# The channel layer of a three-stage kernel by seven block products instead of eight, with the weights' sums on GpSimd and a new order of the program

## Chip, cores and metric

One core of a Trainium2 chip. The metric is the device time of one execution in microseconds (us). The kernel before takes 362.83 us (median of three runs, 362.69 to 362.89).

## The reference

Three stages follow each other on a batch of 2 sequences of 768 tokens with 512 features (8 heads of 64).

```python
# stage 1: retention, by head
state = gamma * state + k_t v_t^T ;  y_t = scale * q_t state
# stage 2: mixing of tokens, then the channel layer
theta = x @ w_theta
y = w_tok_r @ (x * cos(theta)) + w_tok_i @ (x * sin(theta))
u = x + y
x = u + maximum(u @ w_ch, 0)
# stage 3: gated block
h = gelu(x @ w_in) ;  u, v = halves of h
v_n = (v - mean) / sqrt(var + 1e-6) * g_ln
gated = u * (w_sg @ v_n + b_sg)
out = x + gated @ w_out
```

The line that the change works on is `u @ w_ch`.

## The kernel before

**Numbers.** Every operand of a large product is split into two parts of type fp32r, a high half (ScalarE copies the tile, `split_hi`, L339) and a low half (VectorE subtracts the high half from the tile, `split_lo`, L345). `terms3` (which calls `mm`, L319) makes one product of three matmuls: high by high, low by high, high by low.

**Tiling.** Tokens stand in the columns. Group 0 is the first 512 tokens of batch 0, group 1 the first 512 of batch 1, group 2 the last 256 of both. The features are four tiles of 128 rows, so x (`xa` for groups 0 and 1, `xb` for group 2) has tiles (g, d) of 128 x 512. A call of `layer` makes one output tile of 128 x 512 from four input tiles: 4 x 3 = 12 matmuls of 512 columns into one of 8 PSUM banks.

**Stages in the code.** `retention` works through 12 chunks of 128 tokens (scores, mask, outer product, state, attend), `theta` makes the angle and z = x cos, x sin of a chunk, `mix_main` and `mix_rest` mix the tokens (`mix_main` the first 512 columns, in four banks, with matmuls of 512 columns; `mix_rest` the last 256, with matmuls of 256 columns). The last chunk's `mix_main` is followed by `add` (L830), which makes u, and by the halves of u (`split_x` into `uhl`). `channels` is the channel layer, one call of `layer` for each group and feature tile, then `relu` (L908) and the halves of the result (`x2hl`). `up_four`, `up_u` and `up_v` are the first layer of stage 3, `gate_tile` the mixing with w_sg, `finish_four` and `finish` the last layer.

**Seven products.** `up_four` and `finish_four` make the tiles of groups 0 and 1 of their layers by `seven`: the weights (two blocks of input features by two of output features) and the tokens (two blocks of input features by groups 0 and 1) form a 2 x 2 block product. `sum_weights` forms four sums of weight blocks (VectorE, L1138), `sum_tokens` four differences of token tiles for each of two tile numbers (VectorE, L1158), each with its two halves. `seven` makes seven products of 6 matmuls each in four banks, `both` (ScalarE L1202, VectorE L1207) adds two of them into a buffer, and three more adds give the other results.

**Order of the work.** Every step is recorded as an operation of an engine with what it reads and writes. The list `ORDER` gives the sequence, `Plan.schedule` assigns the buffers in that sequence and the instructions are issued in it, each engine in its own order. SP issues all loads and stores but one (`load_half` L465, `weight` L400, the decays are issued by ScalarE). `weight` loads 1 MB of a weight pair and prepares it: L411 on ScalarE, L421 and L431 on VectorE, then the two halves. Before `WARM` a few small matmuls on the identity keep PE busy in its planned gaps (`keep_warm`).

Of the kernel before, what the change touches and what calls it, by code (L numbers as in the profile page):

```python
# [14 lines left out]
ALU = mybir.AluOpType  # L15
# [50 lines left out]
class Plan:  # L66
# [105 lines left out]


ORDER = [
# [52 lines left out]
]  # L227


# [1 line left out]
def retention_spectral_gmlp(  # L231
# [579 lines left out]
    def mix_main(b, s, prio):  # L811
# [14 lines left out]
        if s == NCH - 1:  # L826
            for d in range(NP):

                def add(d=d):
                    V.tensor_tensor(  # L830
                        out=x_tile(b, d), in0=ap(y[b, d]), in1=x_tile(b, d), op=ALU.add
                    )

                t = prio + 1 + d * 0.1
                dve(512, add, ps=True, r=[y[b, d]], w=x_keys(b, d), prio=t)
                split_x(uhl, b, d, t + 1 + LATE * (1 - b))

    def mix_rest(b, s, prio):
        i = b * NCH + s
# [59 lines left out]

    x2hl = {}  # L900

    def channels(g, e, prio):

        t = layer(W_CH, uhl, g, e, prio)

        def relu():
            u = x_tile(g, e)
            V.scalar_tensor_tensor(  # L908
                out=u, in0=ap(t), scalar=0.0, in1=u, op0=ALU.max, op1=ALU.add
            )  # L910

        dve(512, relu, ps=True, r=[t], w=x_keys(g, e), prio=prio)
        split_x(x2hl, g, e, prio)

    def gelu(t, o, prio, ps=True):

# [198 lines left out]
    def sum_weights(base, prio):  # L1115
# [17 lines left out]
            (lambda: block(0, 1), lambda: s3(1), ALU.subtract, [1]),  # L1133
        ]
        for i, (x, y, op, of) in enumerate(pairs):
            dve(
                512,
                lambda i=i, x=x, y=y, op=op: V.tensor_tensor(out=s3(i), in0=x(), in1=y(), op=op),  # L1138
                r=[plain[base][1], plain[base + 1][1], *(sums[n] for n in of)],
                w=[sums[i]],  # L1140
                prio=prio,
            )
            res.append(pair())
            split(res[i], lambda i=i: ap(sums[i]), 512, prio, [sums[i]])
# [90 lines left out]
        dma(256, put, r=[o], prio=prio)  # L1235

    def up_four(j, ws, ts, prio):
        z, x, y, u, v = seven(W_INU, x2hl, ws, ts, j, prio)
        for g, f, part in ((0, j, z), (1, j, x), (0, 2 + j, y), (1, 2 + j, v)):
            if f % 2 == 0:  # L1240
                gu[g, f], gu[g, f + 1] = halves()
            t = part
            if part is not z:
                t = v if part is v else Buf()
                dve(
                    512,
                    lambda t=t, part=part: V.tensor_tensor(
                        out=ap(t), in0=ap(part), in1=ap(u), op=ALU.add
                    ),
                    ps=part is not v, r=[part, u], w=[t], prio=prio,  # L1250
                )
            gelu(t, gu[g, f], prio, ps=part is z)

    def finish_four(j, ws, ts, prio):
        z, x, y, u, v = seven(W_OUT, ghl, ws, ts, j, prio)
# [94 lines left out]
    for k in range(2):  # L1350
        weight(W_INU + k, t - 10 + 5 * k)
        weight(W_INV + k, t + 30 + 5 * k)
    for g in range(3):
        for e in range(NP):
            channels(g, e, t)
            t += 2.7
    ws = sum_weights(W_INU, t - 8)
    ts = sum_tokens(lambda g, d: (lambda: x_tile(g, d), x_keys(g, d)), t - 4)
    for f in range(NP):
# [144 lines left out]
```

## Time and profile before

| | |
|---|---|
| median of the runs | 362.83 us |
| the profiled execution's own time | 362.86 us |
| its span (first to last instruction) | 361.1 us |
| PE (matmul) busy | 356.1 us, 99%, 2308 instructions |
| VectorE (DVE) busy | 295.5 us, 82%, 476 |
| ScalarE (ACT) busy | 187.0 us, 52%, 314 |
| GpSimd (POOL) busy | 9.0 us, 3%, 18 |
| moved by DMA | 44.33 MB |
| granted TensorE clock | 1.00 throughout |

Busy times are unions of the instructions' times on one engine. Matmuls overlap each other, and their ends are modelled, so PE's busy share says that PE always has something under way and not at which pace; the pace is read from the starts. A row of a group names the code line, the engine, the operation, what it writes and reads, the count, the busy time and the mean time of one in ns, and the idle time before it with what ended it.

### The profile page before, as it was taken

What the parts mean: (1) busy time and instruction counts of PE and PEld (TensorE: products, weight loads), DVE (VectorE), ACT (ScalarE), POOL (GpSimd) and SP (SyncE); (2) the same over time, 40 slices, a digit from 0 to 9 for tenths busy, and PEclk for the clock granted to TensorE, in tenths of its full rate; (3) what the DMA queues carried; (4) which work ended last, traced back from release to release, by engine and by line L of the source; (5) the groups of instructions that cost most, each with busy time, mean ns of one, the idle gap of its engine ahead of it and who ended that gap; (6) DMA issues with size and microseconds to landing.
All of it is one profiled execution on the core that took longest, in us unless ns stands there. A gap on an engine that the chain in (4) does not pass through costs nothing.

```text
span 361.1 us, 5762 instructions
## 1 busy us (share of the span) xinstructions
PE 356.1 (99%) x2308; PEld 305.0 (84%) x2308; DVE 295.5 (82%) x476; ACT 187.0 (52%) x314; POOL 9.0 (3%) x18
## 2 busy tenths in 40 slices
PE   8999999999999999999999999999999999999996
PEld 8878888888999888889988888888888889988885
DVE  2799989899478798952788788799899979989984
ACT  1689895545255458524532365465588651342310
POOL 1110000010001000002000000000000000000000
DMA  7999675435773155056023000011000000000224
GB/s 297 416 408 414 259 238 214 182 116 175 239 269 141 54 193 159 0 218 235 0 118 116 0 2 0 0 30 60 0 0 3 0 1 2 2 0 0 72 104 174
DMA packets 13946, 44.33 MB, mean 123 GB/s; under 512 B 1760, under 2 KB 5344, under 8 KB 11488
## 3 DMA queue, kind: packets, MB, share of 16 engines
q1 hardware_dynamic: 13776, 43.92, 33.2%
q8 instruction: 18, 0.29, 0.3%
q14 instruction: 8, 0.07, 0.1%
q10 hardware_dynamic: 144, 0.05, 0.1%
HBM read 38.19 MB, written 5.77 MB: 122 GB/s over the span
## 4 chain that ended last, share of the span: by engine, by line
PE 93%; DMA 4%; DVE 1%; ACT 1%; issue 0%
PE banks L319 93%; DMA xb<-wts 3%; DMA dec<-decays 1%; DVE xb L431 0%; DVE b L345 0%; ACT xb L411 0%; ACT b L339 0%; PE banks L760 0%; DVE b L1311 0%
## 5 line engine op out<-in xcount | busy, mean ns | idle before, releaser
L319 PE MATMUL banks<-b,b 128*128 128x512 f32 (+2 forms) x1764 | 323.0, 350 | 0.5 <-DVE b L345 0.5
L319 PEld LDWEIGHTS banks<-b,b 128*128 128x128 f32 (+1 forms) x1764 | 274.2, 183 | 47.3 <-issue 1.9
L339 ACT ACTIVATE b<-b 128x512 fp32r<-128x512 f32 (+1 forms) x83 | 63.4, 788 | 72.0 <-PE banks L319 26.4
L345 DVE TENSOR_TENSOR b<-b,b 128x512 fp32r<-128x512 f32 (+1 forms) x83 | 70.8, 873 | 14.4 <-ACT b L339 8.9
L345 DVE TENSOR_TENSOR b<-xa,b 128x512 fp32r<-128x512 f32 (+1 forms) x26 | 18.5, 726 | 10.2 <-ACT b L339 10.2
L339 ACT ACTIVATE b<-xa 128x512 fp32r<-128x512 f32 (+1 forms) x26 | 16.9, 663 | 14.0 <-DVE xa L908 5.6
L511 DVE TENSOR_TENSOR b<-banks,causal 128x512 f32<-128x512 f32 x24 | 16.2, 684 | 7.1 <-PE banks L319 7.1
L411 ACT ACTIVATE b<-b 128x1024 f32<-128x1024 f32 x16 | 18.2, 1149 | 5.0 <-DMA b<-wts 4.9
L431 DVE SCALAR_TENSOR_TENSOR b<-b 128x1024 int32<-128x1024 int32 x16 | 19.7, 1228 | 1.2 <-ACT b L411 0.9
L319 PE MATMUL banks<-b 64*128 64x128 f32 (+1 forms) x352 | 19.4, 256 | 0.2
L319 PEld LDWEIGHTS banks<-b 64*128 64x128 f32 (+1 forms) x352 | 17.3, 165 | 2.2 <-DMA b<-qkv 0.8
L938 ACT ACTIVATE b<-b 128x512 f32<-128x512 f32 x24 | 14.6, 627 | 6.7 <-DVE b L928 6.7
L534 ACT ACTIVATE b<-b,dec 128x64 f32<-128x64 f32 x56 | 14.1, 335 | 6.4 <-DMA b<-qkv 6.4
L920 ACT ACTIVATE b<-banks 128x512 f32<-128x512 f32 x18 | 10.2, 589 | 9.3 <-PE banks L319 9.1
L928 DVE SCALAR_TENSOR_TENSOR b<-b,banks 128x512 f32<-128x512 f32 x18 | 12.1, 678 | 2.1 <-ACT b L920 1.9
L421 DVE TENSOR_SCALAR b<-b 128x1024 int32<-128x1024 int32 x16 | 11.0, 686 | 3.2 <-DMA b<-wts 3.2
L339 ACT ACTIVATE b<-xb 128x512 fp32r<-128x512 f32 (+1 forms) x13 | 8.4, 665 | 9.5 <-DVE xb L866 7.8
L782 DVE TENSOR_TENSOR b<-b,b 128x512 f32<-128x512 f32 x20 | 13.2, 680 | 0.1
L716 ACT ACTIVATE b<-banks 128x512 int32<-128x512 f32 x12 | 7.1, 589 | 11.8 <-PE banks L319 11.8
L1029 ACT ACTIVATE b<-b,rstd 128x512 f32<-128x512 f32 x12 | 9.6, 806 | 5.7 <-DVE rstd L1018 5.7
L944 DVE SCALAR_TENSOR_TENSOR b<-b,banks 128x512 f32<-128x512 f32 x18 | 11.9, 679 | 0.6 <-ACT b L938 0.4
L1202 ACT ACTIVATE b<-banks 128x512 f32<-128x512 f32 x8 | 4.7, 593 | 14.2 <-PE banks L319 13.0
(75 smaller groups left out, 217.6 us busy)
## 6 DMA issues: line engine op xcount, KB each, us to landing
b<-wts SPq DMA_DIRECT2D x16, 1024.0 KB, 5.1
b<-qkv SPq DMA_DIRECT2D x24, 512.0 KB, 9.7
out<-b SPq DMA_DIRECT2D x11, 256.0 KB, 2.1
scr<-b SPq DMA_DIRECT2D x5, 512.0 KB, 4.6
b<-scr SPq DMA_DIRECT2D x20, 128.0 KB, 3.1
b<-wsg SPq DMA_DIRECT2D x9, 256.0 KB, 7.4
xa<-wts SPq DMA_DIRECT2D x2, 1024.0 KB, 11.9
xb<-wts SPq DMA_DIRECT2D x1, 1024.0 KB, 10.6
```

What stands on the lines that cost most here:

```text
L319: nc.tensor.matmul(out=o, lhsT=l, rhs=r, start=start, stop=stop, skip_group_check=more)
L339: act(words, lambda: A.activation(out=hi(), in_=src(), func=AF.Copy), prio=prio, r=r, **k)
L345: lambda: E.tensor_tensor(out=lo(), in0=src(), in1=hi().bitcast(F32), op=ALU.subtract),
L411: lambda: A.activation(out=words(1).bitcast(F32), in_=words(1).bitcast(F32), func=AF.Prelu, scale=REBIAS, alpha=SIGN_UP,),
L421: lambda: V.tensor_scalar(out=words(0), in0=words(0), scalar1=29, scalar2=None, op0=ALU.logical_shift_right),
L431: lambda: V.scalar_tensor_tensor(out=words(0), in0=words(1), scalar=3, in1=words(0), op0=ALU.logical_shift_left, op1=ALU.bitwise_or,),
L511: V.tensor_tensor(out=ap(at[i])[:, h * 512 + lo : h * 512 + hi].rearrange("p (n t) -> p n t", n=n), in0=ap(sc[h])[:, lo:hi].rearrange("p ( ...
L534: A.activation(out=v, in_=v, func=AF.Copy, scale=dk[:, h : h + 1])
L782: V.tensor_tensor(out=v, in0=x, in1=v, op=ALU.mult)
L928: lambda: V.scalar_tensor_tensor(out=ap(s), in0=ap(s), scalar=1.0 / GA, in1=ap(t), op0=ALU.add, op1=ALU.mult),
L938: lambda: A.activation(out=ap(s), in_=ap(s), func=AF.Tanh, scale=GA * GC),
L944: lambda: V.scalar_tensor_tensor(out=ap(o), in0=ap(s), scalar=1.0, in1=ap(t), op0=ALU.add, op1=ALU.mult),
```

## The change

1. The channel layer of groups 0 and 1 is made by `seven` too, as `channels_four`; group 2 stays with `channels`. The adds after `seven` move to a helper `sums_of` that `up_four` uses as well. `relu` becomes a function of its own.
2. The halves of u of batch 1 are made only for the feature tiles 2 and 3 (`seven` doesn't use the other two).
3. The four sums in `sum_weights`, now called for three layers, are formed by GpSimd (`pool`, G.tensor_tensor) instead of VectorE.
4. `ORDER` is another list (1059 operations instead of 1007).

```diff
@@ ORDER
-    48, 50, 62, 49, 63, 105, 51, 106, 0, 52, 168, 118, 64, 53, 119, 55, 54, 56, 6, 67, 58, 57, 66,
...
+    48, 49, 50, 55, 52, 56, 118, 63, 62, 105, 106, 119, 51, 0, 120, 53, 54, 168, 58, 64, 181, 67,
...
@@ mix_main
-                split_x(uhl, b, d, t + 1 + LATE * (1 - b))
+                if b == 0 or d >= 2:
+                    split_x(uhl, b, d, t + 1 + LATE * (1 - b))
@@ channels
+    def relu(g, e, t, ps, prio):
+        u = x_tile(g, e)
+        dve(
+            512,
+            lambda: V.scalar_tensor_tensor(
+                out=u, in0=ap(t), scalar=0.0, in1=u, op0=ALU.max, op1=ALU.add
+            ),
+            ps=ps, r=[t], w=x_keys(g, e), prio=prio,
+        )
+        split_x(x2hl, g, e, prio)
+
     def channels(g, e, prio):
...
+        relu(g, e, layer(W_CH, uhl, g, e, prio), True, prio)
+
+    def channels_four(j, ws, ts, prio):
+        for g, e, t, ps in sums_of(seven(W_CH, uhl, ws, ts, j, prio), j, prio):
+            relu(g, e, t, ps, prio)
+
+    def sums_of(parts, j, prio):
+
+        z, x, y, u, v = parts
+        yield 0, j, z, True
+        for g, e, part in ((1, j, x), (0, 2 + j, y), (1, 2 + j, v)):
+            t = v if part is v else Buf()
+            dve(
+                512,
+                lambda t=t, part=part: V.tensor_tensor(
+                    out=ap(t), in0=ap(part), in1=ap(u), op=ALU.add
+                ),
+                ps=part is not v, r=[part, u], w=[t], prio=prio,
+            )
+            yield g, e, t, False
@@ sum_weights
-            dve(
+            pool(
                 512,
-                lambda i=i, x=x, y=y, op=op: V.tensor_tensor(out=s3(i), in0=x(), in1=y(), op=op),
+                lambda i=i, x=x, y=y, op=op: G.tensor_tensor(out=s3(i), in0=x(), in1=y(), op=op),
@@ the main program
-    for g in range(3):
-        for e in range(NP):
-            channels(g, e, t)
-            t += 2.7
+    ws = sum_weights(W_CH, t - 30)
+    ts = sum_tokens(lambda g, d: (lambda: x_tile(g, d), x_keys(g, d)), t)
+    for j in range(2):
+        channels_four(j, ws, ts, t)
+        t += 9.5
+    for e in range(NP):
+        channels(B, e, t)
+        t += 2.7
```

What the new list does to the order shows at three places. Line numbers of the changed kernel are 4 to 25 higher there.

**SP, the first loads.** `b<-qkv` are the halves of retention chunks, `xb<-wts` is the first pair of theta weights (it lands in the space of xb), `dq` the query decays. Before:

```order
L465 DMA b_102<-qkv 128x1024
L465 DMA b_105<-qkv 128x1024
L465 DMA b_107<-qkv 128x1024
L465 DMA b_109<-qkv 128x1024
L465 DMA b_111<-qkv 128x1024
L490 DMA dq<-qdecays 128x512
L465 DMA b_114<-qkv 128x1024
L400 DMA xb<-wts 128x2048
```

Now:

```order
L469 DMA b_102<-qkv 128x1024
L469 DMA b_105<-qkv 128x1024
L469 DMA b_107<-qkv 128x1024
L469 DMA b_109<-qkv 128x1024
L469 DMA b_111<-qkv 128x1024
L469 DMA b_113<-qkv 128x1024
L469 DMA b_115<-qkv 128x1024
L469 DMA b_117<-qkv 128x1024
L494 DMA dq<-qdecays 128x512
L404 DMA xb<-wts 128x2048
```

Eight loads of chunks stand ahead of the theta weights where six stood, and the query decays come after all eight.

**PE, the last work ahead of the first theta product.** Rows `banks<-b` of 128x128 are scores, of 64x64 outer products, rows with 64x128 are attends, `banks<-ident,xa` is a transpose, 128x512 is theta. Before:

```order
L319 MATMUL banks<-b_114 64x64 x8
L760 MATMUL banks<-ident,xa_88 128x128 x4
L319 MATMUL banks<-b_111,state_66 64x128 x8
L319 MATMUL banks<-b_200,b_114 64x128 x8
L319 MATMUL banks<-b_128 128x128 x8
L319 MATMUL banks<-b_130 128x128 x8
L319 MATMUL banks<-b_273,b_202 128x512 x2
```

Now:

```order
L323 MATMUL banks<-b_117 64x64 x8
L323 MATMUL banks<-b_107,state_67 64x128 x8
L323 MATMUL banks<-b_176,b_117 64x128 x8
L323 MATMUL banks<-b_146 128x128 x8
L323 MATMUL banks<-b_165 128x128 x8
L323 MATMUL banks<-b_179 128x128 x8
L764 MATMUL banks<-ident,xa_88 128x128 x4
L323 MATMUL banks<-b_327,b_280 128x512 x2
```

Two more scores, one more outer product and one more attend have come ahead of the first theta product.

**DVE, after the last products of main mixing.** L830 (now L834) are the adds that make u, L345 (now L349) low halves, L1183 the new token differences. Before:

```order
L830 TENSOR_TENSOR xa_89<-banks,xa_89 128x512 x2
L345 TENSOR_TENSOR b_1691<-xa_89,b_1691 128x512
L345 TENSOR_TENSOR b_1689<-b_1590,b_1689 128x512
L345 TENSOR_TENSOR b_1705<-b_1541,b_1705 128x512
L830 TENSOR_TENSOR xa_89<-banks,xa_89 128x512
```

Now:

```order
L834 TENSOR_TENSOR xa_89<-banks,xa_89 128x512
L1183 TENSOR_TENSOR b_1666<-xa_89 128x512
L349 TENSOR_TENSOR b_1625<-b_1615,b_1625 128x512
L1183 TENSOR_TENSOR b_1671<-xa_89 128x512
L349 TENSOR_TENSOR b_1669<-b_1666,b_1669 128x512
L349 TENSOR_TENSOR b_1688<-b_1671,b_1688 128x512
L349 TENSOR_TENSOR b_1582<-xa_88,b_1582 128x512
L1183 TENSOR_TENSOR b_1704<-xa_88,b_1623 128x512
```

Where halves of u followed the adds, differences and their halves now stand; the first product on a difference reads `b_1688`.

## Rows read from the trace of the kernel before

**Rows 1.** The page's first part: busy us (share) x instructions of each engine.

```profile
PE 356.1 (99%) x2308; PEld 305.0 (84%) x2308; DVE 295.5 (82%) x476; ACT 187.0 (52%) x314; POOL 9.0 (3%) x18
```

**Rows 2.** The chain that ended last: start us, us, what.

```profile
4.77 10.56 DMA xb<-wts
...
15.36 1.22 ACT xb L411
...
16.60 1.24 DVE xb L431
...
17.86 1.18 ACT b L339
...
19.06 1.24 DVE b L345
...
20.34 18.55 PE banks L319 x226
38.89 0.59 PE banks L760 x4
39.48 318.51 PE banks L319 x1840
357.99 0.02 issue
358.01 0.42 DVE b L1311
```

**Rows 3.** PE's timeline (start us, us), then groups by form (busy us, mean ns).

```profile
199.83 15.35 PE L319 MATMUL banks<-b,b 128*128 128x512 f32 x67
...
L319 PE MATMUL banks<-b,b 128*128 128x512 f32 x1116 | 256.7, 390 | 0.5 <-DVE b L345 0.5
```

**Rows 4.** Groups by form on DVE and ACT, then a pair in DVE's timeline.

```profile
L345 DVE TENSOR_TENSOR b<-b,b 128x512 fp32r<-128x512 f32 x55 | 36.2, 685 | 2.8 <-ACT b L339 2.8
L339 ACT ACTIVATE b<-b 128x512 fp32r<-128x512 f32 x55 | 33.2, 627 | 51.5 <-PE banks L319 16.8 <-DVE b L1106 15.4 <-DVE b L1158 9.2
...
192.77 1.28 DVE L345 TENSOR_TENSOR b<-b,b 128x512 fp32r<-128x512 f32 x2
```

**Rows 5.** Stretches: us, busy us (x) PE, PEld, DVE, ACT, POOL; clock, DMA, GB/s.

```profile
10.00:40.00 30.00, 29.39 (x383) 24.57 (x382) 27.33 (x41) 25.19 (x68) 2.82 (x4) 1.00 1.02 412
...
160.00:260.00 100.00, 100.00 (x510) 85.71 (x509) 78.30 (x134) 48.04 (x80) 2.32 (x2) 1.00 0.17 61
```

**Rows 6.** Timeline, POOL beside DVE, at 48.9 and at 74.2 us.

```profile
48.90 0.61 POOL L578 TENSOR_TENSOR state<-grown,dec 128x256 f32<-128x256 f32 x1 [20.04 <-PE banks L319]
...
74.23 0.68 DVE L345 TENSOR_TENSOR b<-xa,b 128x512 fp32r<-128x512 f32 x1
74.46 0.93 POOL L578 TENSOR_TENSOR state<-grown,dec 128x256 f32<-128x256 f32 x1 [24.95 <-DVE grown L575]
74.83 1.64 DVE L345 TENSOR_TENSOR b<-b,b 128x1024 fp32r<-128x1024 f32 x1
...
77.00 1.21 DVE L345 TENSOR_TENSOR b<-b,b 128x1024 fp32r<-128x1024 f32 x1
```

**Rows 7.** Timeline of the tail, PE's last matmuls of 256 columns.

```profile
355.77 2.20 PE L319 MATMUL banks<-b,b 128*128 128x256 f32 x17
```

**Rows 8.** Timeline of PE in the head (x8 in the order is x16 here).

```profile
5.15 2.06 PE L319 MATMUL banks<-b 64*128 64x128 f32 x32
...
7.16 0.94 PE L319 MATMUL banks<-ident 128*128 128x128 f32 x6
...
8.54 1.14 PE L319 MATMUL banks<-b,b 128*64 128x128 f32 x16
...
20.34 2.56 PE L319 MATMUL banks<-b,b 128*128 128x512 f32 x10 [0.53 <-DVE b L345]
...
28.14 1.09 PE L319 MATMUL banks<-b,state 64*64 64x128 f32 x16
29.16 1.09 PE L319 MATMUL banks<-b,b 128*64 128x128 f32 x16
30.09 0.64 PE L319 MATMUL banks<-b 128*64 128x64 f32 x16
30.65 5.73 PE L319 MATMUL banks<-b,b 128*128 128x512 f32 x24
```

More of the change, by code (lines that the diff above doesn't have):

```diff
@@ L900, in retention_spectral_gmlp @@
     x2hl = {}
-    def channels(g, e, prio):
[L904 to L909, printed above, removed]
-            )
-        dve(512, relu, ps=True, r=[t], w=x_keys(g, e), prio=prio)
-        split_x(x2hl, g, e, prio)
+    def relu(g, e, t, ps, prio):
[8 more added lines that the diff above has]
+        split_x(x2hl, g, e, prio)
+    def channels(g, e, prio):
+        relu(g, e, layer(W_CH, uhl, g, e, prio), True, prio)
[13 more added lines that the diff above has]
+                ps=part is not v, r=[part, u], w=[t], prio=prio,
+            )
+            yield g, e, t, False
     def gelu(t, o, prio, ps=True):
@@ L1237, in up_four @@
     def up_four(j, ws, ts, prio):
-        z, x, y, u, v = seven(W_INU, x2hl, ws, ts, j, prio)
-        for g, f, part in ((0, j, z), (1, j, x), (0, 2 + j, y), (1, 2 + j, v)):
+        for g, f, t, ps in sums_of(seven(W_INU, x2hl, ws, ts, j, prio), j, prio):
             if f % 2 == 0:
                 gu[g, f], gu[g, f + 1] = halves()
[L1242 to L1252, printed above, removed]
+            gelu(t, gu[g, f], prio, ps=ps)
     def finish_four(j, ws, ts, prio):
```

106 rows, old and new, of the table ORDER are left out of this document.

## Prediction, made before the changed kernel was run

> **What bounds the kernel now.** The page's first part comes first: TensorE (PE) is busy for 99% of the span, VectorE (DVE) for 82%, ScalarE for 52%, GpSimd for 3% [rows 1]. The chain that ended last says the same in order of time: from 20.34 us to 357.99 us there is nothing but PE in it, before that the load and the preparation of the first theta weights, after it one DVE add and the store [rows 2]. A busy PE need not be a full PE, so I looked at its pace: 67 matmuls of 512 columns took 15.35 us [rows 3], and with the last one's shown 0.39 us taken off, the 66 steps are 0.227 us each. All 1116 such matmuls at that pace are 253 us [rows 3], and after 20.34 us the trace knows no wait of PE but the 0.53 us that end there [rows 8]. So the reader should see a kernel whose time is (moment at which PE becomes gapless) + (PE's remaining work) + (tail of 361.1 - 357.99 = 3.1 us). The change can gain only by taking away PE work or by making PE gapless earlier, and it can lose by any new wait of PE.
>
> **Fewer products.** The channel layer for groups 0 and 1 was 2 x 4 calls of `layer`, 12 matmuls each, 96 in all. Now it is 2 x 7 products of 6 matmuls, 84. Twelve matmuls of 512 columns go: 12 x 0.227 = **2.72 us** [rows 3]. Group 2 keeps its four `layer` calls, the other layers keep theirs. This is on the path, since PE is.
>
> **What the other engines get for it.** DVE gets 8 token sums and their 8 low halves, loses 2 low halves of u (batch 1, tiles 0 and 1), gets 4 low halves of the weight sums, 4 adds in `both`, 6 in `sums_of`, and loses the 8 weight sums of the two later layers: net 20 instructions of 512 columns. One alone shows 0.68 us, two in a row 1.28 us, so one more costs 0.60 us [rows 4]: 20 x 0.60 = 12.0 us. ScalarE gets 14 copies (8 - 2 + 4 high halves, 4 in `both`) at about 0.63 us [rows 4], 8.8 us, where 48% of PE's section is used [rows 5]; I count nothing for it, and if that cover were gone the chains of `split` would be 0.6 us later each. GpSimd gets 12 sums. Its row has 256 columns, 0.61 us undisturbed [rows 6], so 512 columns are 1.22 us by twice that, and 0.61 us if it were all fixed cost; I take 1.22, 14.7 us in all. Nothing waits for a weight sum at short notice: the order puts each behind its weights and many DVE instructions ahead of its product. SP issues the same number of transfers.
>
> **Is DVE still ahead of PE?** In the stretch from the end of mixing to the first layer's activations (160 to 260 us) PE is busy 100.0 us and DVE 78.3 us [rows 5]. Of the instructions above 24 net fall here (the 4 sums of the output weights that leave DVE lie later): 78.3 + 24 x 0.60 = 92.7 us against a PE stretch of 100 - 2.7 = 97.3 us. That is tight but under. I walked the new order at the places where PE first needs DVE. Take t = 0 at the end of the last product of main mixing. PE then has four groups of 12 matmuls of 256 columns, 12 x 0.12 us each by the tail's row (17 take 2.20 us, the last one's overlap included, [rows 7]), so the first product on a token difference is due at 5.8 us. DVE has the last mixing add, two differences and three low halves up to the one needed, six instructions of 0.60 us, and with ScalarE's copy between they are done at about 4 us. It is 1.8 us early. The second product is due at 10.0 us, its low half stands seven instructions further, at 8.1 us. The channel results of group 2 and the next layer's differences I walked the same way: the margins are 1 to 3 us, the smallest 0.6 us near the end, where the last tile of the gate passes through DVE. The thing that hides the 12 us is thus DVE's idle time; once it is gone, each DVE instruction costs its 0.60 us.
>
> **GpSimd against DVE.** Where a GpSimd product overlapped DVE instructions with two SBUF inputs, both lost time: GpSimd took 0.93 us instead of 0.61, and the DVE instruction behind it 1.64 us instead of 1.21 [rows 6]. So 0.2 to 0.4 us of DVE were lost per GpSimd instruction of 0.61 us, when DVE was two-input work at that moment, and nothing when it read PSUM. For 12 sums of twice the length that is 0 to 12 x 0.8 = 9.6 us of DVE time; I take the middle, and 0 on PE's path as long as the margins above hold. The Trainium skill, SBUF — State Buffer, "Who interferes with whom", speaks against the change here: a DVE instruction with two SBUF inputs and a GpSimd instruction that reads SBUF exclude each other for the whole instruction. By that rule the full 14.7 us could be taken from DVE; the trace agrees in kind (0.43 us lost, in 1.64 against 1.21) but shows only part of each GpSimd instruction overlapped.
>
> **The head.** The order is new everywhere, and the head is where it matters. Before 20.34 us PE has done five score groups, three outer products, one first and two later attends, one transpose and two theta matmuls. By rows a score group is 1.0 us (two from 5.15 to 7.16), an outer product 0.56 (30.09 to 30.65), a later attend 1.95 (28.14 to 30.09), the first about 1.0 (1.14 with its overlap) [rows 8], the transpose 0.59 [rows 2]: 5.0 + 1.7 + 3.9 + 1.0 + 0.6 and 0.45 for two matmuls of theta are 12.6 us of work in the 15.2 us since 5.15, hence 2.6 us of waiting and of matmuls that only keep PE warm. In the new order, seven score groups, four outer products and four attends stand ahead of the first theta product: 7.0 + 2.2 + 1.0 + 5.9 + 0.6 = 16.7 us. The theta weights are now the tenth transfer of SP instead of the eighth: two loads of 0.524 MB more ahead of them, at 412 GB/s [rows 5] 2.55 us. So they land at 15.33 + 2.55 = 17.9, and the same four steps of preparation (1.22 + 1.24 + 1.18 + 1.24 us, [rows 2]) end at 22.9 us. PE, with about 1 us of waiting left for the first loads (they land some 1.27 us apart at that rate), has done its 16.7 us at 22.9. The two meet; I take 23.2 us for the first theta product. PE becomes gapless 2.9 us later, but with 4.1 us more behind it: **gain 1.2 us**. Bounds: 1.6 us if it starts at 22.8, and a loss of 2.6 us if the additional work doesn't fit and PE still has it to do.
>
> **The sum.** -2.72 (products) - 1.2 (head) + 0.3 (the order has 40 changes between forms of matmul instead of 37, at about 0.1 us) + 0.2 (small waits) = -3.4 us. The profiled execution took 362.86 us, its span 361.1, the median of the runs 362.83, so the sum against either is the same to 0.03 us: **359.4 us**.
>
> **Rivals.** (a) *The sum without new waits of weight*, as above: 358.6 to 360.0. (b) *PE waits at some of the thin places*, 0.7 to 2.5 us together, because a margin of 0.6 to 2 us is used up by GpSimd's sums or a late copy: 360.0 to 361.9. For it speaks the 95% that DVE reaches in its stretch, against it that PE waited for DVE only once after 19 us, for 0.53 us, at 82% [rows 8]. (c) *The head gives nothing back*: the theta weights land 2.55 us later and the additional work is stuck behind its own loads and fades, so PE starts late with all still to do. 362.83 - 2.72 and up to 2.6 more: 360.1 to 362.7. Against it: each group's load stands ahead of the weights in SP's order. (d) *Slower: DVE becomes the bound between mixing and the first activations.* Eight of the GpSimd sums lie there, 8 x 1.22 = 9.8 us. If each shuts DVE out for its whole length, DVE needs 92.7 + 9.8 = 102.5 us in a stretch for which PE needs 97.3: 5.2 us of waiting, 359.4 + 5.2 = 364.6 us. It decides from 4.6 us of loss on (97.3 - 92.7), and the kernel is slower once 8.0 are lost. Against it: the rows show 0.43 us lost at the worst, and part of DVE's work there reads PSUM [rows 6]. This is where the rule of the Trainium skill named above would lead if taken in full. (e) *The change doesn't do what it says*: excluded, the order has 1104 matmuls of 512 columns instead of 1116.
>
> **How the numbers follow.** Two runs of this kernel differ by up to 0.2 us; I call 0.2% (0.73 us) what can be told from no change. (a) 0.56, (b) 0.25, (c) 0.09, (d) 0.05, and 0.05 for (b) or (c) grown to a gain of less than 0.73 us. (c) reaches into "same" with a third of its chance. Faster 0.87, same 0.08, slower 0.05. The range runs from 358.6 (head at its best bound, no waits: 362.83 - 2.72 - 1.6 + 0.3 = 358.8, and a little for the transfers) to 361.6, which takes in (a) and most of (b) and (c).
>
> **What would show it.** Right: matmuls of 512 columns 12 fewer, PE's long piece in the chain beginning at 22.8 to 23.5 us and about 6.3 us shorter than the present 337.6; DVE 86% busy; GpSimd sums of 1.2 us and longer where they meet two-input DVE work. Wrong in the sense of (b) or (d): rows of PE idle before `<-DVE b L349` or `<-ACT` between the last mixing product and the gate, (d) with DVE at 100% there. Wrong in the sense of (c): a wait of PE before 24 us for loads or for DVE. The forecast fails if PE's rows show more than 1 us of new waits, or if PE's pace is not 0.227 us.

## The result: 364.58 us, slower by 0.6%

The changed kernel takes **364.58 us** (median of six runs, 364.37 to 366.12), the kernel before 362.81 us (six runs, 362.69 to 362.89). The ratio is 1.0061, 95% interval 1.0041 to 1.0081. The forecast was 359.4 us, its range ended at 361.6: it was wrong in sign. The profiled execution took 364.49 us, its span is 362.5 us.

### The profile after

The page's first part, which answers to [rows 1]:

```profile
PE 354.7 (98%) x2294; PEld 303.9 (84%) x2294; DVE 313.8 (87%) x496; ACT 194.4 (54%) x328; POOL 33.5 (9%) x30
```

TensorE has fewer instructions and less busy time, VectorE exactly the 20 instructions more that were counted. GpSimd is at 9%. None of this looks like a loss. The chain that ended last, where [rows 2] had nothing but PE from 20.34 us on (start us, us, what):

```profile
46.09 136.49 PE banks L323 x894
...
190.99 2.02 DVE b L1183
...
198.96 0.61 DVE b L1232
...
199.61 159.49 PE banks L323 x774
```

The end of the kernel now hangs on VectorE, with one copy of ScalarE, from 182.6 to 199.6 us, and VectorE falls behind from 190.99 us on. PE's timeline in the head and there (the bracket says how long PE was idle, and for whom):

```profile
23.32 5.72 PE L323 MATMUL banks<-b,b 128*128 128x512 f32 x24
...
179.66 16.77 PE L323 MATMUL banks<-b,b 128*128 128x512 f32 x90
199.61 10.77 PE L323 MATMUL banks<-b,b 128*128 128x512 f32 x39 [3.19 <-DVE b L1232]
```

L1232 is the add in `both`. It reads the bank of the fourth of the seven products of the second half of the channel layer, and the last product of that half goes into the same bank. The matmul at 199.61 us should have followed the one at 196.04 us by 0.227 us; it came after 3.58, so 3.35 us are lost. What stood in VectorE's queue ahead of that add, and what GpSimd did meanwhile:

```profile
190.99 2.02 DVE L1183 TENSOR_TENSOR b<-xa,b 128x512 f32<-128x512 f32 x1
192.93 2.02 DVE L349 TENSOR_TENSOR b<-xb,b 128x512 fp32r<-128x512 f32 x1
194.88 3.49 DVE L349 TENSOR_TENSOR b<-b,b 128x512 fp32r<-128x512 f32 x2
198.28 0.68 DVE L871 TENSOR_TENSOR xb<-banks,xb 128x512 f32<-128x512 f32 x1
198.88 0.68 DVE L1232 TENSOR_TENSOR b<-banks,b 128x512 f32<-128x512 f32 x1
...
190.88 1.58 POOL L1163 TENSOR_TENSOR b<-b 128x512 f32<-128x512 f32 x1 [46.97 <-PE banks L323]
192.43 5.39 POOL L1163 TENSOR_TENSOR b<-b,b 128x512 f32<-128x512 f32 x3
```

GpSimd forms the four weight sums of the first layer (W_INU) here. Four VectorE instructions with two SBUF inputs take 7.29 us from 190.99 to 198.28, where four at 0.60 us [rows 4] take 2.4: **4.9 us lost in the queue ahead of the add** (1.34 for each of the first two, 1.1 for each of the others). The first sum ends at 192.46 us and the VectorE instruction beside it at 193.01, the last ones at 197.82 and 198.37: VectorE ends 0.55 us behind the sum both times, about the 0.60 us of one instruction. The sums didn't start when their weights were ready; GpSimd was idle for 46.97 us until a matmul of PE had ended: one of the mixing's last 256 columns, the last reader of the buffer that the first sum writes.

The stretches around it, then the long one of [rows 5] (columns as there):

```profile
195.00:200.00 5.00, 1.81 (x9) 1.19 (x8) 5.00 (x5) 1.01 (x2) 2.73 (x2) 1.00 0.53 187
200.00:205.00 5.00, 5.00 (x17) 3.94 (x16) 4.46 (x8) 3.74 (x8) 0.00 (x0) 0.66 0.06 23
...
160.00:260.00 100.00, 96.81 (x488) 82.55 (x487) 93.28 (x142) 51.33 (x84) 6.78 (x4) 0.98 0.16 56
```

PE is busy for 1.81 of the five microseconds before 200 us, and in the five after that the granted clock is 0.66: from 200.48 us on seven matmuls follow each other at 0.427 us, near half the pace of 0.227, which is the lower of the two levels (1.2 GHz). That is a second loss, priced below at 1.6 us.

### The profile page after: what moved, and what is told of

Read it like the earlier page. It is cut to its first block, busy times and chain, and to the rows that moved or that the text cites. A ratio compares the mean times of both kernels' runs of the same rounds, so it can differ in the third digit from the quotient of the medians.

```text
span 362.5 us, 5787 instructions
## 1 busy us (share of the span) xinstructions
PE 354.7 (98%) x2294; PEld 303.9 (84%) x2294; DVE 313.8 (87%) x496; ACT 194.4 (54%) x328; POOL 33.5 (9%) x30
## 4 chain that ended last, share of the span: by engine, by line
PE 94%; DVE 4%; issue 0%; ACT 0%; DVEq 0%; ACTq 0%
PE banks L323 94%; DVE b L349 2%; DVE b L1183 1%; DVE b L933 1%; DVE xa L911 1%; DVE b L1232 0%; PE banks L764 0%; ACT b L343 0%; DVE xb L871 0%; DVE b L1325 0%; DVE state L281 0%; DVE halfpi L285 0%; DVEq L1232 0%; ACTq L343 0%
## 5 line engine op out<-in xcount | busy, mean ns | idle before, releaser
L343 ACT ACTIVATE b<-b 128x512 fp32r<-128x512 f32 (+1 forms) x95 | 70.3, 768 | 63.4 <-DVE b L1183 20.7
L349 DVE TENSOR_TENSOR b<-b,b 128x512 fp32r<-128x512 f32 (+1 forms) x95 | 80.3, 865 | 11.7 <-ACT b L343 8.4
L1163 POOL TENSOR_TENSOR b<-b,b 128x512 f32<-128x512 f32 x9 | 15.6, 1734 | 118.4 <-DVE b L435 113.5
L343 ACT ACTIVATE b<-xa 128x512 fp32r<-128x512 f32 (+1 forms) x24 | 15.9, 669 | 16.4 <-DVE xa L911 6.8
L349 DVE TENSOR_TENSOR b<-xa,b 128x512 fp32r<-128x512 f32 (+1 forms) x24 | 17.5, 728 | 0.9 <-ACT b L343 0.8
L786 DVE TENSOR_TENSOR b<-b,b 128x512 f32<-128x512 f32 x20 | 15.0, 776 | 1.0 <-ACT b L755 0.6
L582 POOL TENSOR_TENSOR state<-grown,dec 128x256 f32<-128x256 f32 x8 | 8.3, 1036 | 70.1 <-DVE grown L579 70.1
L1227 ACT ACTIVATE b<-banks 128x512 f32<-128x512 f32 x12 | 7.1, 593 | 8.7 <-PE banks L323 8.1
```

The source lines that it names most:

```text
L343: act(words, lambda: A.activation(out=hi(), in_=src(), func=AF.Copy), prio=prio, r=r, **k)
L349: lambda: E.tensor_tensor(out=lo(), in0=src(), in1=hi().bitcast(F32), op=ALU.subtract),
L786: V.tensor_tensor(out=v, in0=x, in1=v, op=ALU.mult)
L1163: lambda i=i, x=x, y=y, op=op: G.tensor_tensor(out=s3(i), in0=x(), in1=y(), op=op),
```

## The experiments

**Theory A**: a sum on GpSimd and a VectorE instruction with two SBUF inputs exclude each other (while one runs, the other stands still). TensorE pays for what is lost in VectorE's queue ahead of something that it needs soon, less the margin there, and then for the clock. **Rivals**: VectorE is overloaded, with GpSimd or without (B); the clock alone (C); only this place or only this sort of GpSimd instruction does it. The kernel before ran beside each group of experiments: 362.77 us for the first eight, 362.91 for the last.

### Only the four sums of this place go back to VectorE

```diff
+            on_dve = base == W_INU
-            pool(
+            (dve if on_dve else pool)(
                 512,
-                lambda i=i, x=x, y=y, op=op: G.tensor_tensor(out=s3(i), in0=x(), in1=y(), op=op),
+                lambda i=i, x=x, y=y, op=op, E=V if on_dve else G: E.tensor_tensor(
+                    out=s3(i), in0=x(), in1=y(), op=op
+                ),
```

> The changed kernel, only the four weight sums of the first layer's u half (the ones GpSimd formed from 190.9 to 197.8 us) are formed by DVE again, at the same place of the order, all buffers the same. Theory A (a GpSimd sum and a DVE instruction with two SBUF inputs exclude each other for the whole instruction): PE's wait of 3.2 us before 199.6 goes, with it the stretch at half clock behind it (1.9 us); DVE has 4 x 0.60 = 2.4 us more to do, of which 0 to 0.5 us reach PE. 359.2 to 360.0 us. Theory B (DVE simply has too much to do there, 20 more instructions): handing it four more makes the wait longer, 365 us or more. Theory C (the stretch is slow for the clock alone, whatever DVE does): the wait of 3.2 us stays, 363 us or more.

Measured: **359.23 us**, ratio 0.9909 (0.9894 to 0.9925). VectorE and PE in its timeline, and after that its stretch from 160 to 260 us:

```profile
191.40 0.68 DVE L1186 TENSOR_TENSOR b<-xa,b 128x512 f32<-128x512 f32 x1
192.00 0.68 DVE L349 TENSOR_TENSOR b<-xb,b 128x512 fp32r<-128x512 f32 x1
...
195.33 0.69 DVE L1235 TENSOR_TENSOR b<-banks,b 128x512 f32<-128x512 f32 x1
...
185.76 20.60 PE L323 MATMUL banks<-b,b 128*128 128x512 f32 x107
```

```profile
160.00:260.00 100.00, 100.00 (x510) 85.69 (x510) 94.88 (x164) 55.16 (x91) 0.00 (x0) 1.00 0.16 56
```

VectorE has four instructions more to do and is done earlier: the same instructions take 0.68 us, the add (L1235 here) starts at 195.33 us, and PE runs through. VectorE's 94.88 us of 100 are enough, so B falls.

### All twelve sums go back to VectorE

The edit is the one above with `on_dve = True`.

> The changed kernel with all twelve weight sums on DVE (part 3 undone, the order of the list kept; some buffers of the last layer come out differently). DVE has 12 x 0.60 = 7.2 us more work than in the changed kernel and is never held up by GpSimd. Theory A: as the run with only four of them on DVE or up to 1 us slower, 359.2 to 361 us, for the other eight sums stand where DVE has some 20% idle. Theory B: 366 us or more.

Measured: **359.11 us**, ratio 0.9896 (0.9882 to 0.9911), a little under the interval expected, and the best of all kernels here. The other eight sums cost nothing on GpSimd and bring nothing: 0.12 us between the two medians. The page's first part of this kernel:

```profile
PE 352.7 (99%) x2294; PEld 302.5 (85%) x2294; DVE 312.4 (87%) x508; ACT 194.4 (54%) x328; POOL 12.8 (4%) x18
```

VectorE is busy for 312.4 us with 508 instructions, in the changed kernel for 313.8 us with 496. **Taking twelve instructions off VectorE has made it busier.**

### The kernel before, with its sums on GpSimd

```diff
@@ sum_weights of the kernel before
-            dve(
+            pool(
                 512,
-                lambda i=i, x=x, y=y, op=op: V.tensor_tensor(out=s3(i), in0=x(), in1=y(), op=op),
+                lambda i=i, x=x, y=y, op=op: G.tensor_tensor(out=s3(i), in0=x(), in1=y(), op=op),
```

> The kernel before with part 3 of the change alone: the eight weight sums of its two layers by GpSimd, its own order, no seven products in the channel layer. Theory A: each sum holds up one DVE instruction with two SBUF inputs by some 1.3 us where DVE has such work at hand, at most 8 x 1.3 = 10 us of DVE time less the 4.8 us of DVE's own sums; DVE is busy 78 to 82% there, so most is absorbed: 362.5 to 365.5 us, with GpSimd's sums at 1.6 us or more and single DVE instructions of 2 us beside them. Theory B (only the added DVE work counts): DVE has 4.8 us less to do, no loss, 362.2 to 362.9 us.

Measured: 362.84 us, ratio 1.0 (0.9991 to 1.0009): no difference, and inside both expected ranges, so the rows have to decide. The loss is there nevertheless (its timeline):

```profile
151.59 1.52 POOL L1138 TENSOR_TENSOR b<-b 128x512 f32<-128x512 f32 x1 [34.14 <-DVE b L431]
153.06 4.30 POOL L1138 TENSOR_TENSOR b<-b,b 128x512 f32<-128x512 f32 x3
...
307.48 4.96 POOL L1138 TENSOR_TENSOR b<-b,b 128x512 f32<-128x512 f32 x3 [137.32 <-DVE b L431]
...
307.83 3.44 DVE L345 TENSOR_TENSOR b<-b,b 128x512 fp32r<-128x512 f32 x2
311.19 1.80 DVE L1106 TENSOR_TENSOR b<-b,b 128x512 f32<-128x512 f32 x1
312.91 2.62 DVE L345 TENSOR_TENSOR b<-b,b 128x512 fp32r<-128x512 f32 x2
...
299.80 20.55 PE L319 MATMUL banks<-b,b 128*128 128x256 f32 x151
```

Near 310 us VectorE loses (3.44 - 1.28) + (1.80 - 0.68) + (2.62 - 1.28) = 4.6 us, nearly as much as in the changed kernel, and PE waits for nothing: its row runs on from 299.80 to 320.35 us. The loss is nearly the same, the place decides. The first rows also give the sum's own duration, since VectorE stood idle from 151.4 to 156.3 us: 1.4 to 1.5 us, where I had estimated 1.22.

### PE kept busy during the wait

```diff
     for o in plan.schedule(ORDER):
         if o.eng == "PE":
+            if o is plan.ops[595]:
+                keep_warm(7, 13)
```

> The changed kernel with 13 small matmuls on the identity put on PE right before the product that waits 3.2 us (bank 7, which nothing uses at that time); they are no part of the result. They take about 3 us of the wait. If the half clock behind the wait (eight matmuls of 512 columns at 0.427 us instead of 0.227) comes from the wait, the granted clock stays 1.00 and the time falls by 1.6 to 1.9 us to 362.6 to 363.0; the wait for DVE stays where it is. If the half clock has another cause, or if the small matmuls only delay the product, 364.5 us or more.

Measured: 363.15 us, ratio 1.0011 (1.0002 to 1.0021), a little above the interval expected; 1.43 us of the changed kernel's time are back. Its stretch behind the wait, and the last long piece of its chain:

```profile
200.00:205.00 5.00, 4.72 (x22) 3.75 (x21) 4.90 (x9) 4.61 (x9) 0.00 (x0) 1.00 0.21 90
```

```profile
200.47 157.88 PE banks L323 x774
```

The clock stays at 1.00, and the same 774 matmuls take 157.88 instead of 159.49 us. So **1.6 us of the loss were the clock**, a consequence of the wait. C falls: most of the loss remains with the clock kept.

### Two of the four sums on GpSimd

The edit is the first one with `on_dve = base == W_INU and i in (1, 3)`.

> The changed kernel with two of the four W_INU sums on GpSimd (those that ran first, at 190.88 and 192.43 us) and the other two by VectorE at their places in its order. Theory A: two VectorE instructions are shut out, about 1.34 us each, 2.7 us together; in the changed kernel 5.0 us of loss made 3.35 us of waiting, so 1.6 us were margin; a wait of about 1.1 us remains: 360.2 us, up to 362.1 us if the clock falls behind it as it did behind 3.35 us. If the loss went with the number of sums in proportion, half of 5.35 us: 361.9 us. If all four are needed to lose anything (VectorE overloaded, not shut out): 359.1 to 359.5 us.

Measured: **360.21 us** (0.993, 0.9916 to 0.9945). Its timeline, and its stretch behind the wait:

```profile
191.40 2.02 DVE L1186 TENSOR_TENSOR b<-xa,b 128x512 f32<-128x512 f32 x1
193.34 2.02 DVE L349 TENSOR_TENSOR b<-xb,b 128x512 fp32r<-128x512 f32 x1
...
191.29 1.58 POOL L1164 TENSOR_TENSOR b<-b 128x512 f32<-128x512 f32 x1 [46.98 <-PE banks L323]
192.83 1.98 POOL L1164 TENSOR_TENSOR b<-b,b 128x512 f32<-128x512 f32 x1
...
197.81 12.53 PE L323 MATMUL banks<-b,b 128*128 128x512 f32 x54 [0.97 <-DVE b L1235]
```

```profile
200.00:205.00 5.00, 5.00 (x24) 4.14 (x23) 4.90 (x9) 2.36 (x5) 0.00 (x0) 1.00 0.16 23
```

Two sums shut out two instructions, 1.34 us each, 2.7 together; the wait is 0.97 us. The sums end at 192.87 and 194.81 us, the two VectorE instructions at 193.42 and 195.36, again 0.55 us behind: VectorE loses the time that the sum beside it still has to run. The margin is thus 1.7 us here and 4.9 - 3.35 = 1.6 us in the changed kernel: loss minus margin, not a share of the loss. After 0.97 us of waiting the clock did not fall.

### The sums later

The four sums are held back until VectorE has written the sum of the first pair of products, which the expectation calls a difference (a small GpSimd instruction reads it first).

```diff
+    sums = [plan.ops[k] for k in (633, 627, 630, 636)]
...
+        if o is sums[0]:
+            written = [b for b in plan.ops[588].bufs if b.of == "one"][0]
+            G.tensor_scalar(
+                out=gcol, in0=ap(written)[:, 0:4], scalar1=0.5, scalar2=None, op0=ALU.mult
+            )
```

> The changed kernel with its four W_INU sums still on GpSimd, but held back until VectorE has written the first difference that the layer's products wait for (a four-column GpSimd instruction reads that difference first); they then start near 197 us instead of 190.9. Theory A (a GpSimd sum and a VectorE instruction with two SBUF inputs exclude each other, wherever they meet; what it costs is the margin that is used up at that place): the 3.35 us wait at 196.3 and the half clock behind it are gone, the VectorE rows from 197 to 204 us with two SBUF inputs take about 2.0 us instead of 0.68, about 5 us are lost there as before, and TensorE waits somewhere behind for 0 to 3 us: 359.2 to 363.0 us. Theory P (only the place near 191 us was bad, the sums run for nothing elsewhere): no VectorE row near the sums is longer than 0.8 us, 359.2 to 359.6 us. If the place made no difference: 364.0 to 364.8 us.

Measured: 360.2 us (0.9933, 0.9919 to 0.9948). VectorE and PE in its timeline, the waits of PE (us in total, times, longest), and two pieces of its chain:

```profile
199.24 1.65 DVE L349 TENSOR_TENSOR b<-xb,b 128x512 fp32r<-128x512 f32 x1
200.81 2.00 DVE L933 TENSOR_TENSOR b<-b,b 128x512 f32<-128x512 f32 x1
202.74 1.79 DVE L349 TENSOR_TENSOR b<-b,b 128x512 fp32r<-128x512 f32 x1
...
211.19 5.06 PE L323 MATMUL banks<-b,b 128*128 128x512 f32 x21 [0.65 <-DVE b L349]
```

```profile
PE banks L323 <- DVE b L349: 1.2, 2, 0.6
```

```profile
88.61 7.95 DMA scr<-b
...
97.93 99.25 PE banks L323 x650
```

The exclusion goes with the sums, so the place near 191 us is nothing special. Here 3.4 us are lost in three instructions (1.65 + 2.00 + 1.79 less three times 0.68). Of PE's two waits for VectorE only the one at 211.19 us lies behind the sums: 0.81 us in its starts and 0.11 in the next one. Against 359.23 us the median is 1.0 us longer, which this wait covers. The other wait ends at 97.93 us, long before the sums, behind a transfer; the kernel with one operand below has one like it at 98.4 us. In both the profiled execution is the longest of the four (here 360.91 us, the others 360.16 to 360.21), so that wait is probably not in the median.

### The sums in place, VectorE's order changed

In `ORDER` the add that frees the bank (592) and the add of mixing (482) go ahead of two low halves (647, 644) that are needed later:

```diff
-643, 591, 481, 647, 644, 586, 482, 633, 592, 485,
+643, 591, 592, 481, 586, 482, 647, 644, 633, 485,
```

> The changed kernel with all its GpSimd sums in place and another order on VectorE at this one place: the add that frees the bank TensorE waits for (L1232) and the add of mixing (L871) stand ahead of the two low halves of the next layer's differences (L349) instead of behind them. Theory A (each GpSimd sum shuts out one VectorE instruction with two SBUF inputs; TensorE pays only for what stands in VectorE's queue ahead of something it needs): only two shut-out instructions stand ahead of the add, it starts near 194.9 us and TensorE needs the bank at 196.3, so the 3.35 us wait and the half clock behind it are gone; the other two are still shut out, 1.3 us each, behind the add, and may cost 0 to 1.2 us further on as they did when the sums came later: 359.2 to 360.6 us. Rival (the sums cost what they take from VectorE wherever its queue puts the add): the wait only moves, 362.5 to 364.6 us.

Measured: **360.07 us** (0.992, 0.9904 to 0.9937). Its timeline:

```profile
191.43 2.02 DVE L1183 TENSOR_TENSOR b<-xa,b 128x512 f32<-128x512 f32 x1
193.37 2.02 DVE L349 TENSOR_TENSOR b<-xb,b 128x512 fp32r<-128x512 f32 x1
195.31 0.68 DVE L1232 TENSOR_TENSOR b<-banks,b 128x512 f32<-128x512 f32 x1
195.91 0.68 DVE L871 TENSOR_TENSOR xb<-banks,xb 128x512 f32<-128x512 f32 x1
196.51 3.01 DVE L349 TENSOR_TENSOR b<-b,b 128x512 fp32r<-128x512 f32 x3
...
192.86 5.51 POOL L1163 TENSOR_TENSOR b<-b,b 128x512 f32<-128x512 f32 x3
...
179.74 35.44 PE L323 MATMUL banks<-b,b 128*128 128x256 f32 x171
```

All sums are still on GpSimd at the same time, and PE runs through. The two adds that read PSUM take 0.68 us beside a sum, so only three instructions are shut out and one sum costs VectorE nothing. The gain against the changed kernel is 4.5 us, by order alone. Of the 0.8 us that are missing to the first experiment, PE's starts show two gaps of 0.2 us, which end at 202.8 and 210.6 us, each with the next start 0.1 us late, 0.6 us together; the rest stays open.

### What in the GpSimd instruction shuts VectorE out

Two kernels replace the four sums: in one each is an instruction that reads one operand (the second one is left out), in the other two fills with zeros that read nothing (the sums are left out).

```diff
-G.tensor_tensor(out=s3(i), in0=x(), in1=y(), op=op)
+G.tensor_scalar(out=s3(i), in0=x(), scalar1=1.0, scalar2=None, op0=ALU.mult)
```

> The changed kernel with each of the four W_INU sums replaced by a GpSimd instruction of the same 512 columns that reads one operand (a multiplication by 1.0) and writes the sum's tile; the second operand of the four sums is left out. Theory A in the form that GpSimd's reading of SBUF is what shuts out VectorE's second input: the rows of 2.0 us stay, 363.0 to 364.8 us (a one-input instruction may be shorter: 0.3 us of column time less each gives about 1.2 us less). Rival (the exclusion needs two inputs on both engines): VectorE's rows stay at 0.68 us, 359.1 to 359.6 us.

```diff
-G.tensor_tensor(out=s3(i), in0=x(), in1=y(), op=op)
+[G.memset(s3(i), 0.0) for _ in range(2)][-1]
```

> The changed kernel with each of the four W_INU sums replaced by two GpSimd instructions that read nothing and fill the sum's tile with zeros; the values of the four sums are left out. Theory A in the form that GpSimd's reading is what shuts out VectorE's second input: nothing is shut out, VectorE's rows stay at 0.68 us, 359.1 to 359.6 us. Rival (any GpSimd instruction on SBUF, its writing too, shuts VectorE out): rows longer than 1 us while the fills run, at least 1 us of waiting, 360.3 to 364.5 us.

Measured: 359.62 us (0.9916, 0.9901 to 0.9931) with one operand, 359.39 us (0.9909, 0.9892 to 0.9925) with none. The timeline with one operand:

```profile
192.09 6.69 POOL L1164 TENSOR_SCALAR b<-b 128x512 f32<-128x512 f32 x4 [46.99 <-PE banks L323]
...
192.18 1.14 DVE L1187 TENSOR_TENSOR b<-xa,b 128x512 f32<-128x512 f32 x1
193.24 0.68 DVE L349 TENSOR_TENSOR b<-xb,b 128x512 fp32r<-128x512 f32 x1
193.84 1.75 DVE L349 TENSOR_TENSOR b<-b,b 128x512 fp32r<-128x512 f32 x2
```

and with none:

```profile
192.26 3.22 POOL L1164 MEMSET b<- 128x512 f32 x6 [0.21 <-PE banks L323]
...
192.28 1.28 DVE L349 TENSOR_TENSOR b<-b,b 128x512 fp32r<-128x512 f32 x2
```

Without a read nothing is lost, so the loss goes with GpSimd's reading (the operation changes with the number of operands here, and no run separates the two). With one operand, neither expectation was right: the VectorE instruction that starts beside a GpSimd instruction loses 0.46 us, not 1.34. The first is done at 193.32 us, while the GpSimd instruction beside it, at 1.67 us each, runs to about 193.7, so VectorE does not wait for its end. Ahead of the add 0.9 us are lost, under the margin of 1.6. The Trainium skill, SBUF — State Buffer, "Who interferes with whom", calls the contention of the two engines an exclusive lock and says that a VectorE instruction with two SBUF inputs collides with GpSimd instructions that read SBUF and not with those that only write it. By that rule one operand should have been enough for a full exclusion; the runs agree for none and for two, and show a third of the loss for one.

## Why the prediction was wrong, step by step

- **Fewer products** and **the head** were right. The first theta product starts at 23.32 us (predicted 23.2). In the kernel with all sums on VectorE it starts at 23.27 and PE is done at 354.21: 330.9 us against 357.99 - 20.34 = 337.6 before, 6.7 less (predicted 6.3). Without the loss the change gives 362.77 - 359.11 = 3.66 us; the sum said 3.4.
- **VectorE's count** was right: 20 instructions more, and 94.88 us in the stretch with four sums that I had given to GpSimd (4 x 0.60 us less is 92.5; predicted 92.7).
- **"Nothing waits for a weight sum at short notice"** is where it failed. That is true and beside the point: nobody waited for a sum; a sum kept VectorE from an add that PE was waiting for. I asked who needs the new instruction, not whom it holds up while it runs. I also placed the sums behind their weights, while the buffers they write came free only at 190.8 us.
- **"I take the middle, and 0 on PE's path as long as the margins above hold"** failed with it. The loss was 4.9 us for four sums, 1.2 each, above the 0.8 I had as the upper end: that end came from a GpSimd row in [rows 6] that VectorE's two-input work met for only a part, and from 1.22 us for a sum that takes 1.4 to 1.5 alone and up to 2.0 here. Read as the time that GpSimd still has to run, that row had the price already: 74.46 + 0.93 - 74.83 = 0.56 us to run, 0.43 lost; here 192.46 - 190.99 = 1.47 to run, 1.34 lost. Over all twelve sums the loss, estimated from the busy times, is 313.8 - (312.4 - 12 x 0.60) = 8.6 us, inside the 0 to 9.6 of the prediction; what it had wrong is that more than half of it falls in a row ahead of one add with a margin of 1.6 us.
- **The walk of margins** followed the differences, their halves and the results of group 2, and not the adds of `both` that free PSUM banks. The place where PE waited was not in it.
- **The clock** was no term of the sum. The wait of 3.35 us brought 1.6 us more: 3.35 + 1.6 of the 5.35 us that lie between 359.23 and 364.58. The remaining 0.4 us were not traced.
- **Rival (d)** had 364.6 us and the cause in kind, with a chance of 0.05. Its reckoning was another one: VectorE is not the bound of the stretch (93.28 us of 100 busy, the sums' cost in it), and a comparison of totals would never have shown the loss, which lies in a queue at one place. In the same way (b) had the mechanism, a thin place, and too small a price.

## What to carry to other kernels

Before work goes from VectorE to GpSimd, look at which VectorE instructions will run beside it: a GpSimd instruction with two SBUF operands beside two-SBUF-input work took 1.0 to 1.34 us from VectorE here, more than the 0.60 us it was to save. Price it as the time that the GpSimd instruction still has to run. It hurts where something PE needs stands behind it in VectorE's queue, and only by what exceeds the margin there. So look for such an add that frees a bank, put it ahead of work that is not urgent, or place the GpSimd work beside instructions that read PSUM. Sums on VectorE (359.11 us) beat both kernels.

## What was not expected of the hardware

- How much a GpSimd instruction of 512 columns took from a VectorE instruction with two SBUF inputs went with its own operands: 1.0 to 1.34 us with two, about 0.46 with one, 0 with none. The sums themselves took 1.6 to 2.0 us beside VectorE and 1.4 to 1.5 alone. VectorE's instructions with one operand in PSUM stayed at 0.68 us beside a sum.
- Work given to GpSimd didn't lighten VectorE: eight sums moved in the kernel before leave its busy time at 295.4 us (295.5 in [rows 1]), twelve in the changed kernel raise it from 312.4 to 313.8.
- After 3.35 us without matmuls the granted clock fell to its lower level; after 0.97 us it stayed. It fell only once PE was at work again: the first three matmuls took 0.87 us together, the next seven 0.427 us each.
